# Normalised, transposed tokens of two segments kept in DRAM and read back, in place of making them a second time

## Chip, cores, metric

One core of one Trainium2 chip. The metric is the device time of one execution in microseconds (us), the median of several executions. A profile is of one execution of the same program and runs some 1.7 us shorter in its span than the measured time.

## The reference, cut to what matters

```python
x = A_x                                   # 2048 tokens x 1024
xn = _layernorm(x, axis=-1)
return x + _A_ref(xn, wq, wk, wv, wo, beta) + _B_ref(xn, w1, b1, w2, b2)
# A: 32 heads of 32; four segments of 512 tokens; in each, causal softmax attention
#    plus a read of a running memory M, z:  q, k, v = xn @ wq, xn @ wk, xn @ wv
# B: an MLP over the token axis: y = gelu(layernorm(xn)^T w1 + b1) w2 + b2
```

## The kernel before

The stages are: norm and first hidden products (to some 35 us), w1 (to some 180 us), w2 (to some 373 us) and attention (to the end). K of segments three and four is made in the w2 stage, between products of w2, from tokens that are scaled to f16 and transposed by DMA into `xnK`. In attention the same tokens are loaded from x, scaled and transposed again, in bf16, into `xnT`, for Q and V.

```python
def k_prepare(self, i, p):                       # called after each product of the w2 stage
    n = 7 * i + self.ORDER.index(p)
    if n in self.TOKENS_AT:                      # (2, 3, 4, 6, 8, 9, 10, 11)
        m = self.TOKENS_AT.index(n)
        c = 8 + m
        self.xn_scale(c, F16)
        self.fw.dma(self.xnK[m // 4][...], self.xs[c % 4][:].bitcast(F16), ..., transpose=True, own=True)
    if n - 2 in self.TOKENS_AT[:4]:
        self.xn_load(12 + self.TOKENS_AT.index(n - 2))
    n -= 7 * (self.K_FIRST - 1)
    if 1 <= n < 5:                               # the third of these overwrites half of xnK[1] in place
        self.differences(self.kB, self.R_kB, self.kD, self.R_kD, (n,))
    ...

def xn_load(self, c):                            # 256 KB of x
def xn_scale(self, c, dtype=BF16):               # DVE: (x - mean) * rstd, in place
def xn_transpose(self, c):                       # DMA transpose into xnT[s % 2]
```

Attention runs in 32 units. PE's work is cut into "dense" stretches (projections) between the logits and the weighing of the unit before; the DVE work of a unit is a queue of side steps, of which one is taken at certain stops of the dense stretches. When a job of eight matmuls is complete, `end(b)` empties its PSUM bank, and this too is mostly DVE work. Two banks alternate (6 and 7), so a job can't start before the job two back has been emptied.

```python
XN_AT = (0, 1, 2, 3, 6, 7, 8, 9, 14, 15, 16, 17)     # units with a token step
for u in range(N_UNIT):
    ...
    if u:
        self.weigh(u - 1, 2)
        self.side.append(...)                        # scales of unit u - 1
    if N_GRP <= u:
        self.side.append(lambda u=u: self.phi_q(u))
    self.side.extend(steps)                          # products, add, transpose of the output
    if u + 1 < N_UNIT:
        self.side.append(lambda u=u: (self.phi_k(u + 1), self.k_transpose(u + 1)))
    if xn is not None:
        self.side.append(lambda c=xn: (self.xn_scale(c), self.xn_transpose(c), ...))
    ...

def dense(self, n, side=True):
    ...                                              # matmuls of the job up to the next stop
        if stop == 8:
            end(b)                                   # e.g. kT <- PSUM, fin <- PSUM (DVE)
            self.jobs.popleft()
        elif self.side and stop in stops:
            self.side.popleft()()
```

Of the kernel before, what the change touches and what calls it, by code (L numbers as in the profile page):

```python
# [9 lines left out]
F16 = mybir.dt.float16  # L10
# [7 lines left out]
SEG_L = 512  # L18
F_MLP = 3584
P = 128  # L20
N_TCH = S_TOK // P
N_DCH = D_MODEL // P
# [364 lines left out]
class _Kernel:  # L387
# [508 lines left out]
    def alloc_w2_rest(self):  # L896
        w = _Walk(self.mem, self.B_AT + self.STG_AT, self.B_AT + self.S2_AT)
        self.stg, self.R_stg = [], []
        for k in range(4):
            t, r = w.take(f"stg{k}", [P, D_MODEL], BF16, 2)  # L900
            self.stg.append(t)
            self.R_stg.append(r)
        self.xs, self.R_xs = [], []
        self.take_xs(w, 1)
        w = _Walk(self.mem, self.B_AT + self.K_AT, self.B_AT + self.FREE_AT)
        self.take_xs(w, 3)
        self.wkp, self.R_wkp = [None] * 2, [None] * 2
        self.wkp[0], (self.R_wkp[0],) = w.take("wkp0", [P, N_DCH, 2 * P], BF16)
        self.sk, self.R_sk = w.take("sumk", [P, 4, N_DCH // 2, P], F16, 4)
        for k in range(2):  # L910
            self.load_stg(k)
        for m in range(4):
            self.xn_load(8 + m)
        self.alloc_w2(1)
        self.load_w2(1)
        self.load_wkp(0)
        w = _Walk(self.mem, self.B_AT + self.FREE_AT, self.SB_END - self.SB_BASE)
        self.xnK, self.R_xnK = [], []
        for k in range(2):
            t, r = w.take(f"xnK{k}", [P, N_DCH, SEG_L], F16, 4)  # L920
            self.xnK.append(t)
            self.R_xnK.append(r)
        self.kB = [[self.xnK[c][:, 4 * k:4 * k + 4, :] for c in range(2)] for k in range(2)]
        self.R_kB = [[self.R_xnK[c] for c in range(2)] for _ in range(2)]
        self.kD, self.R_kD = [], []
        for k in (0, 1, 3):
            t, r = w.take(f"kD{k}", [P, N_DCH // 2, SEG_L], F16)
            self.kD.append(t[:])
            self.R_kD.append(r)
        self.kD.insert(2, self.kB[0][1])  # L930
        self.R_kD.insert(2, self.R_kB[0][1])
        self.k_d = self.nc.dram_tensor("k_part", (N_UNIT // 2, P, SEG_L), BF16).ap()
        self.R_kd = [Res(f"kd{u}") for u in range(N_UNIT // 2)]
        self.pk_d = self.nc.dram_tensor("pk_part", (N_GRP, P, SEG_L), BF16).ap()
        self.R_pkd = [Res(f"pkd{u}") for u in range(N_GRP)]
# [105 lines left out]
    def k_prepare(self, i, p):  # L1041

        n = 7 * i + self.ORDER.index(p)
        if n in self.TOKENS_AT:
# [3 lines that stand above are left out]
            self.fw.dma(self.xnK[m // 4][:, :, (m % 4) * P:(m % 4 + 1) * P], self.xs[c % 4][:].bitcast(F16),  # L1048
                        reads=[self.R_xs[c % 4]], writes=[self.R_xnK[m // 4][m % 4]], transpose=True, own=True)
        if n - 2 in self.TOKENS_AT[:4]:  # L1050
            self.xn_load(12 + self.TOKENS_AT.index(n - 2))
        n -= 7 * (self.K_FIRST - 1)
        if 1 <= n < 5:
            self.differences(self.kB, self.R_kB, self.kD, self.R_kD, (n,))
        elif n == 5:
            self.alloc_kout()
        n, g = n % 7, n // 7
        if 0 <= g < self.N_KP and n == 6:
            self.pair_sums(("k", g), (1, 2))
        if i == self.N_W2 - 1 and n < 2:  # L1060
            for c in (2 * n, 2 * n + 1):
                self.xn_scale(c)
                self.xn_transpose(c)
# [57 lines left out]

    def put_out(self, c, t, R):
        self.fw.dma(self.part_d[:, c, :], t[:].bitcast(F16), reads=R, writes=[self.R_out[c]], is_output=True)

    def xn_load(self, c):
        self.fw.dma(self.xs[c % 4][:], self.x_d[:, c, :], writes=[self.R_xs[c % 4]])
# [141 lines left out]
    def proj_job(self, ring, u, end):  # L1268
        s = u // N_GRP

        def mm(b, i):
            self.fw.mm(self.bank(b), ring.slots[u % 2][:, i, :], self.xnT[s % 2][:, i, :], start=(i == 0), stop=(i == 7))

        def finish(b):
            if u + 2 < N_UNIT:
                ring.ensure(u + 2)
            end(b)

        return [0, None, lambda: [ring.res[u % 2]] + self.R_xnT[s % 2], mm, finish, ring is self.wk_ring]

    def v_job(self, m, c):
        s, bv, i = m // 2, m % 2, m % 3

        def mm(b, dc):
            self.fw.mm(self.bank(b), self.xnT[s % 2][:, dc, c * P:(c + 1) * P], self.wv[:, dc, bv * 512:(bv + 1) * 512],
                       start=(dc == 0), stop=(dc == 7))

        def end(b):
            dst, src = self.vA[i][:, c, :, 0:D_HEAD], self.bank(b).rearrange("p (h d) -> p h d", d=D_HEAD)
            if m in (1, 2):  # L1290
                self.fw.op("dve", lambda e: e.tensor_copy(dst, src), reads=[self.R_bank[b]], writes=[self.R_vA[i][c]])
            else:
                self.fw.op("act", lambda e: e.activation(dst, src, ACT.Copy), reads=[self.R_bank[b]],  # L1293
                           writes=[self.R_vA[i][c]])

        return [0, None, lambda: [self.R_wv[bv], self.R_xnT[s % 2][c]], mm, end, m in (1, 2)]

    def wo_job(self, c, half):
        s = c // 4
# [194 lines left out]
    QUOTA_FROM, QUOTA = 18, (24, 20)  # L1494
    STOPS = ((1, 4, 7), (1, 4))
    STOPS_FEW = ((1, 3, 5, 7), (1, 3, 5))
    XN_AT = (0, 1, 2, 3, 6, 7, 8, 9, 14, 15, 16, 17)

    def unit_jobs(self, u):
        jobs = [self.wo_job(*self.wo_jobs.popleft())] if 10 <= u < self.QUOTA_FROM else []  # L1500
# [22 lines left out]
    def attention(self):  # L1523
# [11 lines left out]
        for u in range(N_UNIT):  # L1535
            if u == N_GRP:
                t, R = _Walk(self.mem, self.B_AT + self.STG_AT, self.B_AT + self.S2_AT).take(
                    "oT2", [P, N_GRP, SEG_L], BF16, N_GRP)
                self.oT.append(t)
                self.R_oT.append(R)  # L1540
                self.load_fin(0)
                self.load_fin(1)
            if 1 <= u <= N_GRP:
                self.fw.dma(self.wo[:, u - 1, :], self.A_wo[(u - 1) * P:u * P, :], writes=[self.R_wo[u - 1]])
            even = u % 2 == 0
            self.jobs.extend(self.unit_jobs(u))
            total = 8 * len(self.jobs) - sum(j[0] for j in self.jobs) - self.left
            xn = self.XN_AT.index(u) + 4 if u in self.XN_AT else None
            if u in self.XN_AT[::4]:
                self.xn_load(xn)  # L1550
                self.xn_load(xn + 1)
            if u >= 18 and even:
                cuts = self.cut(total, (0, 5, 1, 4, 0, 9, 5))
            elif u < 10 or u >= 14 and total <= 26:
                cuts = self.cut(total, (0, 4, 2, 4, 1, 13, 8) if even else (7, 3, 2, 4, 1, 15))
            else:
                cuts = self.cut(total, (0, 4, 2, 2, 2, 14, 8) if even else (7, 3, 2, 2, 2, 16))
            end = u >= N_UNIT - 4
            self.stops = self.STOPS_FEW if total <= 26 and u >= 14 else self.STOPS
            self.dense(cuts[0])  # L1560
            self.logits(u, 0)
            self.dense(cuts[1], end)
            while end and self.side:
                self.side.popleft()()
            if u:
                self.weigh(u - 1, 0)
            self.dense(cuts[2], False)
            if u:
                self.weigh(u - 1, 1)
            self.dense(cuts[3], False)  # L1570
            if u:
                self.weigh(u - 1, 2)
                steps = self.combine(u - 1)
                last = steps[-1]
                steps[-1] = lambda u=u, last=last: (last(), self.o_transpose_dma(u - 1))
                self.side.append(steps.pop(0))
# [3 lines that stand above are left out]
                self.side.extend(steps)  # L1580
# [3 lines that stand above are left out]
                self.side.append(lambda c=xn: (self.xn_scale(c), self.xn_transpose(c), c % 4 < 2 and self.xn_load(c + 2)))  # L1584
            self.dense(cuts[4])
            self.logits(u, 1)
            if even:
                self.dense(cuts[5])
                self.logits(u, 2)
            self.dense(8 * len(self.jobs) - sum(j[0] for j in self.jobs) - self.left)  # L1590
# [87 lines left out]
```

## Time and profile before

| | before |
|---|---|
| time, median of 6 runs | 652.26 us (652.11 to 652.52) |
| PE busy, clock | 645.9 us, full |
| DVE busy | 433.7 us |
| DMA share, 200 to 250 us | 0.78 |
| DMA share, 450 to 500 and 500 to 550 us | 0.60, 0.69 |

PE is the bound nearly everywhere (94% of the chain that ended last); DVE comes next, with 41.6 and 43.8 us of 50 in two stretches of attention. The lines are in the prediction.

### The profile page before, as it was taken

To read this page: it belongs to the slowest core of one execution; us is meant where nothing else is said; L and a number is where in the kernel's file an instruction comes from. 1 tells how busy PE (TensorE), PEld (TensorE's weight loads), DVE (VectorE), ACT (ScalarE), POOL (GpSimd) and SP (SyncE) were. 2 spreads that over 40 slices of the span, in tenths; PEclk is the share of its full clock that TensorE was granted. 3 is DMA by queue.
4 is the path that set the end of the run, shared out by engine and by line. 5 is a ranking of instruction groups with operands and counts; after the bars stand their busy time and mean duration, and the time that the engine had idled before them with its cause. 6 is when DMAs were issued, how large, how long until landed. Compare 5 with 4: busy or idle time off the path is not lost.

```text
span 650.5 us, 11182 instructions
## 1 busy us (share of the span) xinstructions
PE 645.9 (99%) x4611; PEld 303.6 (47%) x4611; DVE 433.7 (67%) x808; ACT 281.4 (43%) x305; POOL 154.2 (24%) x179
## 2 busy tenths in 40 slices
PE   9999999999999999999999999999999999999998
PEld 3444444444444444444444444444544454445544
DVE  6975676665555664744638325767887888777896
ACT  7543232232210000111101047778767778889770
POOL 2500000000011220220202203343334444554440
PEclk9999999999999999999999999999999999999999
DMA  9804233242498947538262957979654677435434
GB/s 303 216 0 130 65 107 88 64 116 79 127 261 193 238 120 210 157 102 231 79 208 96 263 130 177 184 168 227 134 135 98 155 165 139 112 98 128 105 94 139
DMA packets 190123, 95.00 MB, mean 146 GB/s; under 512 B 108664, under 2 KB 176248, under 8 KB 190072
## 3 DMA queue, kind: packets, MB, share of 16 engines
q1 hardware_dynamic: 189928, 94.25, 57.2%
q8 instruction: 36, 0.59, 0.4%
q14 instruction: 15, 0.12, 0.1%
q10 hardware_dynamic: 144, 0.03, 0.0%
HBM read 69.23 MB, written 11.53 MB: 124 GB/s over the span
## 4 chain that ended last, share of the span: by engine, by line
PE 94%; DVE 3%; ACT 2%; issue 1%; DMA 0%; POOL 0%; DVEq 0%
PE ps_all L199 94%; ACT pT L1364 1%; DVE prod L1465 1%; DVE ln_st L587 1%; DMA xin<-in_A_x_dram 0%; DVE h L627 0%; DVE ost L1418 0%; POOL ln_rs L611 0%; DVE mtmp L1230 0%; DVE kT L1262 0%; DVE fin L1307 0%; DVE mtmp L1228 0%; ACT qT L1253 0%; ACT vA L1293 0%; DVE ln_mv L590 0%
## 5 line engine op out<-in xcount | busy, mean ns | idle before, releaser
L1364 ACT ACTIVATE pT<-ps_all 128x2048 bf16<-128x2048 f32 x80 | 150.2, 1877 | 47.4 <-PE ps_all L199 46.9
L1368 POOL TENSOR_SCALAR_AFFINE_SELECT pT<-pT 128x512 bf16<-128x512 bf16 x128 | 105.6, 843 | 160.7 <-ACT pT L1364 160.7
L689 DVE TENSOR_TENSOR part<-ps_all,part 128x512 f32<-128x512 f32 x84 | 57.7, 690 | 108.2 <-PE ps_all L199 87.8
L1075 POOL TENSOR_TENSOR part<-part,stg 128x512 f32<-128x512 f32 x24 | 33.0, 1404 | 285.1 <-DVE part L689 285.1
L199 PE MATMUL ps_all<-wv,xnT 128*128 128x512 bf16 x256 | 68.5, 380 | 0.4 <-ACT qT L1253 0.2
L746 ACT ACTIVATE g<-part,b1c 128x512 f16<-128x512 f32 x36 | 26.0, 722 | 98.8 <-DVE part L689 98.8
L199 PE MATMUL ps_all<-xnT,wq 128*128 128x512 bf16 x256 | 66.4, 380 | 0.0
L199 PE MATMUL ps_all<-wo,oT 128*128 128x512 bf16 (+2 forms) x272 | 63.8, 367 | 0.0
L694 ACT ACTIVATE part<-ps_all 128x512 f32<-128x512 f32 x24 | 14.0, 596 | 101.1 <-PE ps_all L199 67.1
L1418 DVE TENSOR_TENSOR ost<-ps_all,eps 128x396 bf16<-128x396 f32 (+1 forms) x72 | 37.2, 522 | 28.5 <-PE ps_all L199 27.8
L199 PEld LDWEIGHTS ps_all<-vA,pT 128*128 128x128 bf16 x1280 | 45.7, 96 | 20.4 <-DVE ost L1418 1.7
L199 PE MATMUL ps_all<-g,sum 128*128 128x512 f16 x224 | 51.0, 379 | 0.0
L199 PE MATMUL ps_all<-g,w2s 128*128 128x512 f16 x224 | 51.0, 379 | 0.0
L199 PE MATMUL ps_all<-gT,sum 128*128 128x512 f16 x224 | 50.3, 379 | 0.0
L199 PE MATMUL ps_all<-vA,pT 128*128 128x33 bf16 x1280 | 48.5, 177 | 0.3 <-DVE ost L1418 0.3
L199 PE MATMUL ps_all<-h,sum 128*128 128x512 f16 x192 | 45.2, 379 | 0.0
L199 PE MATMUL ps_all<-h,w1s 128*128 128x512 f16 x192 | 44.9, 379 | 0.0
L199 PE MATMUL ps_all<-hT,sum 128*128 128x512 f16 x192 | 43.6, 379 | 0.0
L199 PEld LDWEIGHTS ps_all<-wo,oT 128*128 128x128 bf16 x272 | 23.9, 98 | 24.4 <-issue 3.7
L199 PEld LDWEIGHTS ps_all<-xnT,wq 128*128 128x128 bf16 x256 | 22.6, 97 | 25.4 <-issue 5.3
L199 PEld LDWEIGHTS ps_all<-g,sum 128*128 128x128 f16 x224 | 21.9, 98 | 26.4
L199 PEld LDWEIGHTS ps_all<-g,w2s 128*128 128x128 bf16 x224 | 21.9, 98 | 26.4
(118 smaller groups left out, 875.1 us busy)
## 6 DMA issues: line engine op xcount, KB each, us to landing
w2s<-in_B_w_dram SPq DMA_DIRECT2D x8, 1792.0 KB, 9.5
w1s<-in_B_w_dram SPq DMA_DIRECT2D x12, 1024.0 KB, 5.6
wq<-in_A_wq_dram SPq DMA_DIRECT2D x32, 256.0 KB, 3.3
xs<-in_A_x_dram SPq DMA_DIRECT2D x24, 256.0 KB, 3.4
stg<-in_A_x_dram SPq DMA_DIRECT2D x16, 256.0 KB, 2.9
out_dram<-stg SPq DMA_DIRECT2D x16, 256.0 KB, 3.9
wk<-in_A_wk_dram SPq DMA_DIRECT2D x16, 256.0 KB, 3.6
fin<-out_dram SPq DMA_DIRECT2D x16, 256.0 KB, 3.2
```

Of the source, the lines that this page charges most:

```text
L199: ins = self.nc.tensor.matmul(*args, **kwargs)
L587: fw.op("dve", lambda e: e.bn_stats(st[:, 6 * h:6 * h + 6], src[:, 512 * h:512 * h + 512]), reads=[self.R_xin[c]], writes=[R])
L689: self.fw.op("dve", lambda e: e.tensor_tensor(self.tmp[dst][:], self.bank(b), self.tmp[src][:], op=ALU.add), reads=[self.R_bank[b], self.R ...
L694: self.fw.op("act", lambda e: e.activation(self.tmp[dst][:], self.bank(b), ACT.Copy), reads=[self.R_bank[b]], writes=[self.R_tmp[dst]])
L746: self.fw.op("act", lambda e: e.activation(self.gB[f % 2][half][:, f // 2, :], src, ACT.Gelu_apprx_tanh, bias=self.b1c[:, f:f + 1], scale= ...
L1075: fw.op("pool", lambda e: e.tensor_tensor(self.tmp[t][:], self.tmp[t][:], self.stg[k][:, 512 * half:512 * half + 512], op=ALU.add), reads= ...
L1364: fw.op("act", lambda e: e.activation(dst, src, ACT.Exp, scale=SCALE), reads=self.R_bank[0:4], writes=[R[v % 2][kb] for v, kb, _ in blocks ...
L1368: fw.op("pool", lambda e: e.affine_select(d, d, pattern=[[0, 4], [1, P]], compare_op=ALU.is_ge, fill=0.0, base=0, channel_multiplier=-1), ...
L1418: fw.op("dve", lambda e: e.tensor_tensor(dst, src, eps, op=ALU.add), reads=[self.R_bank[b], self.R_eps], writes=[self.R_ost[o][part]])
L1465: fw.op("dve", lambda e: e.tensor_tensor(self.prod[:], ost[:, :, 0:D_HEAD], rec.unsqueeze(2).to_broadcast([P, 32, D_HEAD]), op=ALU.mult), ...
```

## The change

The intent is to make the tokens of the last two segments once. They lie in `xnK` in f16 already; the change writes them to DRAM (two writes of 1 MB) and replaces eight loads, eight scales and eight DMA transposes of the attention phase by eight plain loads. Q and V of these segments then read f16 tokens against bf16 weights.

```diff
+        if n in (9, 13):
+            k = (n - 9) // 4
+            self.fw.dma(self.xn_d[k], self.xnK[k][:], reads=self.R_xnK[k], writes=[self.R_xnd[k]], is_output=True)
...
+    def xn_of(self, s):
+        t = self.xnT[s % 2][:]
+        return t.bitcast(F16) if s >= 2 else t
+
+    def xn_part(self, s, k):
+        self.fw.dma(self.xn_of(s)[:, 2 * k:2 * k + 2, :], self.xn_d[s - 2, :, 2 * k:2 * k + 2, :], reads=[self.R_xnd[s - 2]],
+                    writes=[self.R_xnT[s % 2][k]], own=True)
...   (q and v jobs read self.xn_of(s) in place of self.xnT[s % 2])
-            if u in self.XN_AT[::4]:
+            if xn == 4:
                 self.xn_load(xn)
                 self.xn_load(xn + 1)
+            for k in (1, 2):
+                if u in self.XN_AT[k]:
+                    self.xn_part(k + 1, self.XN_AT[k].index(u))
```

More of the change, by code (lines that the diff above doesn't have):

```diff
@@ L932, in alloc_w2_rest @@
         self.k_d = self.nc.dram_tensor("k_part", (N_UNIT // 2, P, SEG_L), BF16).ap()
+        self.xn_d = self.nc.dram_tensor("xn_part", (2, P, N_DCH, SEG_L), F16).ap()
+        self.R_xnd = [Res(f"xnd{k}") for k in range(2)]
         self.R_kd = [Res(f"kd{u}") for u in range(N_UNIT // 2)]
@@ L1271, in mm @@
         def mm(b, i):
-            self.fw.mm(self.bank(b), ring.slots[u % 2][:, i, :], self.xnT[s % 2][:, i, :], start=(i == 0), stop=(i == 7))
+            self.fw.mm(self.bank(b), ring.slots[u % 2][:, i, :], self.xn_of(s)[:, i, :], start=(i == 0), stop=(i == 7))
         def finish(b):
@@ L1284, in mm @@
         def mm(b, dc):
-            self.fw.mm(self.bank(b), self.xnT[s % 2][:, dc, c * P:(c + 1) * P], self.wv[:, dc, bv * 512:(bv + 1) * 512],
+            self.fw.mm(self.bank(b), self.xn_of(s)[:, dc, c * P:(c + 1) * P], self.wv[:, dc, bv * 512:(bv + 1) * 512],
                        start=(dc == 0), stop=(dc == 7))
@@ L1294, in end @@
                            writes=[self.R_vA[i][c]])
-        return [0, None, lambda: [self.R_wv[bv], self.R_xnT[s % 2][c]], mm, end, m in (1, 2)]
+        return [0, None, lambda: [self.R_wv[bv]] + (self.R_xnT[s % 2][c:c + 1] if s < 2 else self.R_xnT[s % 2]), mm, end, m in (1, 2)]
     def wo_job(self, c, half):
@@ L1496 @@
     STOPS_FEW = ((1, 3, 5, 7), (1, 3, 5))
-    XN_AT = (0, 1, 2, 3, 6, 7, 8, 9, 14, 15, 16, 17)
+    XN_AT = ((0, 1, 2, 3), (6, 7, 8, 9), (14, 15, 16, 17))
     def unit_jobs(self, u):
@@ L1547, in attention @@
             total = 8 * len(self.jobs) - sum(j[0] for j in self.jobs) - self.left
-            xn = self.XN_AT.index(u) + 4 if u in self.XN_AT else None
-            if u in self.XN_AT[::4]:
+            xn = self.XN_AT[0].index(u) + 4 if u in self.XN_AT[0] else None
+            if xn == 4:
                 self.xn_load(xn)
                 self.xn_load(xn + 1)
+            for k in (1, 2):
+                if u in self.XN_AT[k]:
+                    self.xn_part(k + 1, self.XN_AT[k].index(u))
             if u >= 18 and even:
```

## The prediction

> **What bounds the kernel now.** I read the page's table of busy time first, then the chain that ended last, then a table of stretches of 50 us, then the waits, and last the timeline of the two places that the change touches.
>
> ```profile
> PE 645.9 (99%) x4611; PEld 303.6 (47%) x4611; DVE 433.7 (67%) x808; ACT 281.4 (43%) x305; POOL 154.2 (24%) x179
> ...
> PEclk9999999999999999999999999999999999999999
> ...
> PE 94%; DVE 3%; ACT 2%; issue 1%; DMA 0%; POOL 0%; DVEq 0%
> ...
> L199 PE MATMUL ps_all<-g,sum 128*128 128x512 f16 x224 | 51.0, 379 | 0.0
> L199 PE MATMUL ps_all<-g,w2s 128*128 128x512 f16 x224 | 51.0, 379 | 0.0
> ...
> L199 PEld LDWEIGHTS ps_all<-g,sum 128*128 128x128 f16 x224 | 21.9, 98 | 26.4
> L199 PEld LDWEIGHTS ps_all<-g,w2s 128*128 128x128 bf16 x224 | 21.9, 98 | 26.4
> ```
>
> PE is busy 99% of the span, at the full clock, and 94% of the last chain is PE. The last four lines say something that the change needs: a moving operand in f16 takes the same 379 ns against f16 weights (sum) as against bf16 weights (w2s), and f16 weights load in the same 98 ns as bf16 ones.
>
> The stretches say where PE has any room (columns: stretch, its length, then busy us of PE, PEld, DVE, ACT, POOL, then clock, DMA share, GB/s):
>
> ```profile
> 200.00:250.00 50.00, 50.00 (x234) 22.68 (x232) 29.54 (x35) 2.39 (x4) 8.46 (x6) 1.00 0.78 198
> ...
> 400.00:450.00 50.00, 50.00 (x572) 24.97 (x573) 33.98 (x82) 39.37 (x34) 19.37 (x27) 1.00 0.90 180
> 450.00:500.00 50.00, 49.84 (x501) 24.03 (x500) 41.56 (x84) 37.38 (x36) 18.44 (x23) 1.00 0.60 137
> 500.00:550.00 50.00, 49.81 (x582) 25.27 (x582) 43.84 (x85) 40.25 (x36) 23.71 (x26) 1.00 0.69 152
> ```
>
> The first is the w2 stage beside K, where the writes are added; the other three are the part of the attention phase where the work is taken away. PE idles 0.35 us in the three together. Since a busy PE may still hide short waits, I also summed, over the records, the time from one matmul's start to the next one's less its columns at 2.4 per ns: about 21 us of excess from 350 us to the end, of which some 17 us are the 0.1 us steps into and out of the 32-row logits matmuls, whose number does not change. Single waits above 0.25 us there are only six, 1.8 us together. So all that a faster DVE or DMA could give back is 2 to 4 us of 650.
>
> **What the Trainium skill says.** "TensorE: Matmul & The Clock Gate", section "Back-to-back issue gap", gives N/2.4 + 2.5 ns for a lone warm matmul, 215.8 ns at 512 columns. The trace agrees: groups of 14 such matmuls follow each other every 3.02 us in the w2 stage, 215.7 ns each. (Its faster "sustained" figure of 131 ns is not seen here.) "Perfetto Trace Analysis", section "Identifying the Most-Contended Engine", warns that matmul busy share is no measure of distance to the roofline; hence the check by starts above. "VectorE: DVE Perf Modes", section "The perf-mode tier table", puts tensor_scalar on 16-bit SBUF data in its fastest tier, 693 ns for 2048 elements; here 1024 elements take 543 ns, with f16 or bf16 output alike. "DMA: Bandwidth & Descriptors", section "Measured", has 1 MB in 6.15 us; here the 1024 KB w1s loads land in 5.6 us (median), and the 1792 KB w2s loads in 9.5.
>
> **The change, part by part.** The static order of the two kernels shows the same PE, ACT and POOL instructions in the same order. DVE loses eight instructions and two others move by a place; SP loses six.
>
> 1. Removed from attention: eight DVE scales of xs, 8 x 0.543 = 4.3 us, of DVE's 119 us in 400 to 550. The two places where DVE does hold PE are these:
>
> ```profile
> 482.09 0.69 DVE L1230 SCALAR_TENSOR_TENSOR mtmp<-kT,mtmp 128x512 bf16<-128x512 bf16 x1
> 482.70 0.68 DVE L1262 CAST kT<-ps_all 128x512 bf16<-128x512 f32 x1
> 483.30 1.03 DVE L1418 TENSOR_TENSOR ost<-ps_all,eps 128x396 bf16<-128x396 f32 x2
> ```
>
> The weighing on PE at 483.91 waits 0.3 us for ost, and the same at 503.18. The last scale before them ran at 468.33 and the next at 510.12; after 490.87 DVE even idled 2.25 us before ost. So the scales are not in those queues, and the 4.3 us fall almost wholly beside PE. I give it 0.2 us.
>
> 2. Removed: eight loads of x (256 KB) and eight DMA transposes (256 KB, 1.24 to 2.11 us of SP each); added: eight plain loads of 256 KB. No PE wait in 400 to 550 is put down to a DMA, so this is worth 0 us, maybe 0.1.
>
> 3. Added: two writes of 1 MB in the w2 stage. Here is the queue as it stands, and the DVE steps that depend on it:
>
> ```profile
> 218.48 4.62 SPq L221 DMA_TRANSPOSE xnK<-xs  x3
> 223.15 0.58 SPq L221 DMA_DIRECT2D out_dram<-stg  x1
> 223.78 0.44 SPq L221 DMA_DIRECT2D w2s<-in_B_w_dram  x1
> 224.26 4.42 SPq L221 DMA_DIRECT2D out_dram<-stg  x1
> ```
> ```profile
> 229.35 1.21 DVE L663 TENSOR_TENSOR kD<-xnK,xnK 128x2048 f16<-128x2048 f16 x1
> ...
> 238.70 2.17 DVE L663 TENSOR_TENSOR xnK<-xnK 128x2048 f16<-128x2048 f16 x1
> ...
> 241.45 1.08 DVE L648 TENSOR_TENSOR sum<-sum,w2s 128x1792 f16<-128x1792 f16 x1
> ```
>
> The 16 DMA engines are 0.9 to 1.06 busy from 180 to 230, moving some 240 GB/s, so 1 MB costs about 4.4 us of all of them (an estimate from that rate). The first write goes between the first and second of the last three transposes: the last tokens land near 229.5 in place of 225, just when the difference at 229.35 wants them. The w2s load issued at 223.78 lands 8.5 us later, at 232.3; now near 236.7, ahead of its first reader on DVE at 237.4 and on PE at 243.7. The second write is queued behind it, and lands near 239 to 241. The difference at 238.70 overwrites half of the second xnK in place, so it must now wait for that write to have read it: 0 to 2.5 us. After it, PE next needs a sum made at 241.45 to 242.5, at 247.54 (5 us of room), and the sums for K that end at 247.8, at 250.56 (2.8 us of room). So the expected stall of DVE fits into the room, and PE pays 0; if the write lands 3 to 4 us later than I think, PE pays 1 or 2 us. I give it 0.2 us on average.
>
> 4. Changed type: 128 q matmuls (16 units x 8) get an f16 moving operand with bf16 weights, as g with w2s has: no cost. 128 v matmuls get f16 weights with a bf16 moving operand, a pair that the trace does not have; both types alone are free, so I take 0 us. Sum: -0.2 - 0.1 + 0.2 = -0.1 us.
>
> **The rivals.** (a) The freed DVE and DMA time comes through: waits of ACT and DVE shrink and PE's small gaps close. For it: DVE is at 83 to 88% in 450 to 550. Against: the gaps are 2 to 4 us in all, and those above 0.25 us from 555 on lie after the last removed item (538). It would give 650.5 to 651.5. (b) The writes become a new wait: DMA is the fullest resource just where they are put, and the in-place difference is tied to the second one. PE would stop for 1 to 4 us around 247 to 252: 653.5 to 656. (c) The mixed types cost something at each switch between bf16 logits or weighings and f16 projections, some 6 switches in each of 16 units; at 20 ns, 2 us: 654.5. Nothing in the trace speaks for it, and the f16 stage shows nothing when weights alternate between f16 and bf16. (d) The plain loads must wait for PE to be done with the old tokens and hold up the transposes of oT and pk behind them on SP: each has about a unit (8 us) of room, so I think it hidden.
>
> **Range and chances.** The three runs of before spread by 0.36 us. Rival (a) sets the lower edge, (b) and (c) the upper, which I think somewhat likelier to be touched. A gain of 2% is 13 us, more than all PE waits of the phase, so faster is nearly out of the question; slower by 2% needs a cost of 0.1 us in each of the 128 v matmuls or a wait repeated unit by unit. Predicted 652.3 us, range 650.8 to 654.8; faster 0.01, same 0.96, slower 0.03.
>
> **What would show it.** PE's busy time stays at about 645 us with the same count of matmuls; DVE's falls by 4 to 5 us; the q and v matmuls stay at 380 ns and their starts 216 ns apart; xs has 16 scales in place of 24. In the w2 stage a DVE wait on the second write may appear before the in-place difference, up to 3 us, with no PE wait behind it. I am wrong if PE idles near 247 to 252, if v matmuls with f16 weights start more than 220 ns apart, if PE's clock falls below full, or if a wait on the loads from the kept copy appears at the first v or q job of segments three and four.

## The result, and the profile after

652.6 us median (652.43 to 652.84, 6 runs) against 652.26 us: a ratio of 1.0005, 95% interval 0.9992 to 1.0018. Ratios are the mean time of one kernel's fast runs over that of the other's of the same rounds, so not quite the ratio of the medians.

First the page's busy line of the changed kernel, and its stretches (columns as before):

```profile
PE 645.8 (99%) x4611; PEld 303.2 (47%) x4611; DVE 428.1 (66%) x800; ACT 281.4 (43%) x305; POOL 153.9 (24%) x179
```
```profile
200.00:250.00 50.00, 50.00 (x234) 22.65 (x232) 29.99 (x36) 2.39 (x4) 8.46 (x6) 1.00 0.89 239
...
450.00:500.00 50.00, 49.71 (x504) 24.09 (x501) 39.23 (x81) 37.64 (x37) 17.77 (x23) 1.00 0.50 123
500.00:550.00 50.00, 49.81 (x568) 24.80 (x566) 40.92 (x81) 40.24 (x36) 24.41 (x26) 1.00 0.55 133
```

The work did move: DVE lost 5.6 us, the DMA share fell from 0.60 to 0.50 and from 0.69 to 0.55 where the tokens were made, and rose from 0.78 to 0.89 where they are written. PE did not notice: 645.8 us.

The w2 stage, where I had feared a stall, in the timeline of the changed kernel (start, length, engine, line, operation, tiles):

```profile
231.04 0.32 SPq L221 DMA_DIRECT2D xn_part<-xnK  x1
```
```profile
229.62 1.22 DVE L663 TENSOR_TENSOR kD<-xnK,xnK 128x2048 f16<-128x2048 f16 x1
...
238.96 2.17 DVE L663 TENSOR_TENSOR xnK<-xnK 128x2048 f16<-128x2048 f16 x1
```

Both differences stand 0.27 us later than before, and the whole timeline was shifted by as much since 183 us, before the first write, by a wait of PE on DVE that comes and goes between runs. Behind it stands a w2s load issued at 170 us, which neither kernel changes: in all fourteen profiles PE's first weights of `gT` with `sum` are loaded 5.16 to 5.17 us after it lands, and it lands at 177.87 to 178.50 us (178.05 here before, 178.31 after). So up to 0.6 us between single executions is chance, from this load alone. No wait is shown before either difference. The writes landed 5.5 us after issue (median of the two, the longer 6.0), so the second was through by about 237. The last tokens landed at 226.2 us and the w2s load behind them at 234.1, later than before by 1.3 and 1.8 us.

The changed kernel's profile is 0.6 us longer than the other's. 0.27 us is that shift. The other 0.3 us are here, at 472 us; DVE and PE of the kernel before, then of the changed one:

```profile
472.17 0.68 DVE L1262 CAST kT<-ps_all 128x512 bf16<-128x512 f32 x1
...
473.57 0.59 PE L199 MATMUL ps_all<-wo,oT 128*128 128x512 bf16 x2
```
```profile
472.47 1.00 DVE L1243 SCALAR_TENSOR_TENSOR mtmp<-kT,mtmp 128x512 bf16<-128x512 bf16 x1
...
473.39 0.68 DVE L1275 CAST kT<-ps_all 128x512 bf16<-128x512 f32 x1
...
474.12 0.11 PEld L199 LDWEIGHTS ps_all<-wo,oT 128*128 128x128 bf16 x2 [0.42 <-DVE kT L1275]
474.13 0.61 PE L199 MATMUL ps_all<-wo,oT 128*128 128x512 bf16 x2
```

With one side step fewer in the queue, phi of k was taken one stop earlier, and the copy that empties a bank fell in behind it. It ran 1.2 us later (0.27 of it the shift), and PE waited for the bank: between the start of the last wv matmul and the first wo one lie 0.52 us where 0.22 us stood.

To see whether such a wait lasts to the end, I compared the start of each of PE's 4611 weight loads with the same one of the kernel before. The changed kernel falls behind for good at two places only, by 0.27 us at 182 to 183 us and by 0.31 us at 473.6, and is 0.54 us behind at its last weight load. So the 0.3 us aren't made good later.

### The profile page after: what moved, and what is told of

Same layout as the page of the kernel before. It is cut to its first block, busy times and chain, and to the rows that moved or that the text cites. A ratio compares the mean times of both kernels' runs of the same rounds, so it can differ in the third digit from the quotient of the medians.

```text
span 651.1 us, 11170 instructions
## 1 busy us (share of the span) xinstructions
PE 645.8 (99%) x4611; PEld 303.2 (47%) x4611; DVE 428.1 (66%) x800; ACT 281.4 (43%) x305; POOL 153.9 (24%) x179
## 4 chain that ended last, share of the span: by engine, by line
PE 91%; DVE 5%; ACT 2%; DMA 2%; issue 1%; POOL 0%; DVEq 0%
PE ps_all L199 91%; ACT pT L1377 1%; DMA w2s<-in_B_w_dram 1%; DVE prod L1478 1%; DVE ln_st L587 1%; DVE sum L648 0%; DMA xin<-in_A_x_dram 0%; DVE mtmp L1243 0%; DVE h L627 0%; DVE mtmp L1241 0%; DVE fin L1320 0%; DVE ost L1431 0%; DVE kT L1275 0%; POOL ln_rs L611 0%; DVE part L689 0%
## 5 line engine op out<-in xcount | busy, mean ns | idle before, releaser
L199 PE MATMUL ps_all<-xnT,wq 128*128 128x512 bf16 (+1 forms) x256 | 66.4, 380 | 0.0
L199 PEld LDWEIGHTS ps_all<-gT,sum 128*128 128x128 f16 x224 | 21.8, 98 | 26.8 <-DVE gT L663 0.6
```

The costliest lines, as they stand in the source:

```text
L199: ins = self.nc.tensor.matmul(*args, **kwargs)
```

## The experiments

Kernels are compared only within the same rounds. Where 0.3 us is at stake, the interval of the ratio (about 0.0013 to either side, 0.85 us) cannot carry a verdict; there I rest on single waits in the trace and say so. By the rule of 2% every run here is "the same" as the kernel before; where I write "slower", the interval lies above 1.

### Its place in the queue kept (e1_place), and the pair repeated (after_again, e1_again)

```diff
             if xn is not None:
                 self.side.append(...)
+            elif u in self.XN_AT[1] + self.XN_AT[2]:
+                self.side.append(lambda: None)
```

> The changed kernel, but an empty step stands in the side queue where each removed scale stood, so that DVE's order is that of the kernel before less eight scales (checked: no other difference in order). In the changed kernel one copy of kT out of PSUM slipped behind two other DVE steps and ran at 473.39 where it ran at 472.17 before, and PE waited 0.31 us for that bank at 473.8. Theory (the slipped copy is the cost): the copy is back before those steps, the wait near 474 is gone, and the time is 0.3 us below the changed kernel, 652.2 to 652.4, equal to the kernel before. Rival (the writes or the mixed types cost it): the wait may go, but the time stays at 652.6.

> The changed kernel itself once more, beside the next three on one chip, since 0.3 us is as large as the spread of single runs. Theory (a slipped copy of kT costs 0.3 us): 652.5 to 652.8, 0.2 to 0.4 above the same kernel with its places kept, and the wait of 0.3 us near 474 again. Rival (the 0.3 us was chance): the two within 0.1.

> The changed kernel with its places kept in the side queue, a second time, on the same chip as the changed kernel. Theory: 652.3 within 0.15, equal to the kernel before and 0.2 to 0.4 below the changed kernel. Rival: no difference to the changed kernel.

e1_place: 652.43 us, against 652.36 for the kernel before (ratio 1.0001, 0.9988 to 1.0014). On one chip: the changed kernel 652.61 us (652.49 to 652.86), with the place kept 652.37 us (652.16 to 652.65), the kernel before 652.38 us. In the timeline of e1_place the copy is in front again and the wait is gone:

```profile
472.00 0.68 DVE L1275 CAST kT<-ps_all 128x512 bf16<-128x512 f32 x1
...
473.68 0.59 PE L199 MATMUL ps_all<-wo,oT 128*128 128x512 bf16 x2
```

after_again has the wait a second time:

```profile
473.71 0.11 PEld L199 LDWEIGHTS ps_all<-wo,oT 128*128 128x128 bf16 x2 [0.43 <-DVE kT L1275]
```

The wait is in both traces of the changed kernel and in neither of the two with the place kept. By the starts of weight loads against the kernel before, after_again falls behind by 0.30 us at 473.6 us, and it keeps this to the end; the two with the place kept have no step there and end within 0.06 us of the kernel before. So the slipped copy, which e1 takes away alone, costs PE 0.3 us, and no other cost of the change is seen on PE. (The spans of the four profiles don't show this: 651.1 and 650.7 us for the changed kernel, 650.9 for both with the place kept. The latter two are each the slowest of five executions and took 0.3 us longer behind PE's last work.) The medians fit with 0.2 to 0.3 us, but their intervals overlap.

### The writes alone (e2_writes)

The kernel before with the two writes added in `k_prepare`, and nothing that reads them.

```diff
+        if n in (9, 13):
+            k = (n - 9) // 4
+            self.fw.dma(self.xn_d[k], self.xnK[k][:], ..., is_output=True)
```

> The kernel before with the two 1 MB writes alone; the attention phase is untouched and nobody reads what is written. Theory (the writes fit into the room that DVE and PE have): 652.3, as before, within 0.2, no PE wait between 215 and 260, and the same DVE times to within 0.5 us. Rival (the writes are the cost): 652.6 or more, with a DVE wait before the in-place difference near 239 or a later w2s load that holds DVE.

652.33 us against 652.36 (ratio 0.9999, 0.9987 to 1.0012). The in-place difference began at 238.55 in place of 238.70, with no wait. So two writes cost no time. There was little room to spare: in this execution the second write landed at 238.0 us, half a us before the difference that has to wait for it.

### The types alone (e3_types)

The kernel before, with the eight scales writing f16 and q and v reading `xn_of(s)`.

```diff
-(self.xn_scale(c), self.xn_transpose(c), ...)
+(self.xn_scale(c, F16 if c >= 8 else BF16), self.xn_transpose(c), ...)     # and xn_of(s) in q_job, v_job
```

> The kernel before with tokens of segments three and four scaled to f16 and used as f16 by q and v; loads, scales and transposes stay. Theory (types are free): 652.3 within 0.2; the q and v matmuls of these segments 379 ns, starts 216 ns apart inside a group, weights loaded in 98 ns. Rival (a switch between bf16 and f16 costs some ns): with 20 ns at some 100 switches 2 us more, 654.

652.3 us against 652.36 (ratio 0.9998). The view of the token tile of e3_types shows both pairs of types in one group (nanoseconds are least, median, most):

```profile
L199 PE MATMUL ps_all<-xnT,wq x256: 376/379/390, 373.6 to 617.5; 128*128 128x512 bf16 x64, 128*128 128x512 f16 x64
L199 PEld LDWEIGHTS ps_all<-wv,xnT x256: 95/98/99, 376.9 to 600.8; 128*128 128x128 bf16 x64, 128*128 128x128 f16 x64
L199 PE MATMUL ps_all<-wv,xnT x256: 376/379/390, 377.1 to 601.0; 128*128 128x512 bf16 x128
```

The first two groups are half of each type, and half of the third has f16 weights under its bf16 operand; the spread is 14 ns for matmuls and 4 ns for loads. Starts inside a group follow at 216 ns (median) in v and q, as before. The types cost nothing here.

### The saving alone (e4_loads)

Wrong result: raw x is loaded straight into the token tile, without writes, scales, transposes or f16. (Its output still passed the comparison; so that comparison does not see the attention branch of these segments well.)

```diff
+    def xn_part(self, s, k):
+        self.fw.dma(self.xnT[s % 2][:, 2 * k:2 * k + 2, :]..., self.x_d[:, 4 * s + k, :], ...)
-                self.side.append(lambda c=xn: (self.xn_scale(c), self.xn_transpose(c), ...))     # for c >= 8
+                self.side.append(lambda: None)
```

> WRONG RESULT ON PURPOSE: the eight loads, scales and transposes in attention are replaced by eight plain 256 KB loads of raw x straight into the token tile, in bf16, with empty steps keeping DVE's order; no writes, no f16. The saving of the change alone, without any of its costs. Theory (the removed work lay beside PE): 652.1 to 652.4, at most 0.2 us below before; DVE busy falls by 4.3 us and PE's waits at 483 and 503 stay at 0.3 us each. Rival (the saving is real and the writes or types ate it): 651.5 or less.

652.28 us against 652.36 (ratio 1.0, 0.9986 to 1.0014), with DVE at 428.7 us in place of 433.7. The waits at 483 and 503 are where they were (0.33 us each by matmul starts). So nothing was gained and then eaten: the removed work was never in the time.

### How much room DVE has: copies added (e5_copies1, e5_copies3)

The kernel before, with one or three copies of the token tile onto itself ahead of each of the eight scales.

```diff
+        for _ in range(m if c >= 8 else 0):
+            self.fw.op("dve", lambda e: e.tensor_copy(x[:], x[:]), reads=[R], writes=[R])
```

> The kernel before with three more copies of the token tile onto itself at each of the eight scales of segments three and four: what the change takes away on DVE, fourfold in place of none, 8 x 3 x 0.54 = 13 us more of DVE. Theory (one scale fits into DVE's room of about 1 us, but not four): at the scale at 468 the copy of kT slips by 1.6 us and PE waits some 0.8 us; over all places 1 to 4 us more, 653.3 to 656.3. Rival (DVE has room to spare anywhere): within 0.3 us of before. Rival (DVE work goes into the time one for one): 13 us more, 665.

> The kernel before with one extra copy (some 0.45 us) at each of the eight scales, in place of three, which cost 8.2 us. Theory (a queue with some 0.5 to 1 us of room at each place: what fits costs nothing, what exceeds it costs one for one): the waits of the threefold run, less two copies each, leave 0.2 to 1.2 us: 652.5 to 653.6. Rival (each us of DVE costs 0.6 to 0.8 us from the first on, so that taking the scales away should also have gained): 8 x 0.45 x 0.75 = 2.7 us, 655.

| kernel | DVE busy, us | time, us |
|---|---|---|
| place kept, scales gone (e1_again) | 428.7 | 652.37 |
| before | 433.7 | 652.38 |
| one copy more at each | 437.0 | 653.13 |
| three copies more at each | 444.8 | 660.53 |

The threefold run missed my 653.3 to 656.3: it cost 8.1 us. I had looked at one of the eight places. The list of PE's waits in e5_copies3 shows that three different evacuations came late (us in total, times, longest):

```profile
PE ps_all L199 <- DVE ost L1423: 2.9, 5, 1.1
PE ps_all L199 <- DVE kT L1267: 2.3, 2, 1.7
PE ps_all L199 <- DVE fin L1312: 1.6, 3, 1.0
```

The seven new waits end at 458, 460, 478, 518, 531, 535 and 550 us, so they stand at most of the places and not at one. The single copy then met its forecast (0.2 to 1.2 us expected, 0.7 found against 652.43 us; the interval, 0.9999 to 1.0024, only just takes in 1). By the starts of weight loads 0.40 us of it stand at 473.6, before the same wo matmul that the slipped copy held. The curve bends just above the place where the tuned kernel stands: 5 us of DVE less give nothing, 3.3 us more cost 0.7, the next 7.8 cost 7.4.

### How much room the w2 stage has: writes doubled and trebled (e6_writes2, e6_writes3)

The kernel of e2_writes with each 1 MB written two or three times, to places of their own.

```diff
-            self.fw.dma(self.xn_d[k], self.xnK[k][:], ...)
+            for j in range(m):                       # m = 2, 3
+                self.fw.dma(self.xn_d[m * k + j], self.xnK[k][:], ...)
```

> The kernel before with each of the two 1 MB writes made twice, to separate places. Theory (single writes fit, with at least 3 us to spare): one more MB ahead of the last two transposes and the w2s load moves them by 3.5 to 4.5 us, and DVE's first difference from 229 to 231 to 233; PE loses 0 to 2 us: 652.3 to 654.3. Rival (DMA traffic here is hidden whatever its size): 652.3, no shift on DVE.

> The same with each write three times, 4 MB more than the change writes. Theory: the w2s load that PE needs at 243 lands some 8 us later than with one write, near or after that time, the in-place difference waits for the last write as well, and PE loses 3 to 10 us: 655 to 662. Rival (hidden): 652.3.

Twice: 652.54 us against 652.43 (ratio 1.0001, 0.9986 to 1.0017). Three times: 657.87 us (ratio 1.0088, 1.0074 to 1.0101). DVE of the first, then DVE and PE of the second, in their timelines:

```profile
242.88 1.23 DVE L663 TENSOR_TENSOR xnK<-xnK 128x2048 f16<-128x2048 f16 x1 [3.86 <-DMA xn_part<-xnK]
```
```profile
248.59 1.23 DVE L663 TENSOR_TENSOR xnK<-xnK 128x2048 f16<-128x2048 f16 x1 [8.25 <-DMA xn_part<-xnK]
...
250.63 1.87 PE L199 MATMUL ps_all<-xnK,wkp 128*128 128x512 f16 x4 [3.33 <-DVE stg L1089]
252.29 5.34 PE L199 MATMUL ps_all<-gT,sum 128*128 128x512 f16 x14
```
```profile
245.00:260.00 15.00, 11.67 (x41) 4.58 (x40) 10.16 (x14) 1.19 (x2) 0.00 (x0) 0.77 0.63 191
```

The wait I had drawn is real, and its size is a matter of dose: none with one write, 3.86 us of DVE with two, which its room swallows almost whole, 8.25 us with three, of which 3.33 reach PE. (3.86 us is more than the 2.8 us of room that I had drawn. But the late difference took 1.23 us, where it takes 2.17 beside POOL's add, so what follows it on DVE was only 3.2 us late, and PE fell behind by 0.3 us at 249 to 251.) The first DVE difference did not move at two writes (229.60), against my forecast for it. At three writes the forecast of the time held, but the w2s load landed at 239.2, 4.7 us later than with one write and not 8, so PE's stop came from the late in-place difference and the evacuation behind it.

At three there is a second price. After its wait PE needed 5.34 us for fourteen matmuls that take 3.19 us otherwise, starting 427 ns apart until 256.6 us and 216 ns again from 257, and the clock of the stretch was 0.77: after the stop PE ran for some 6 us at about half its clock. The profile is of the slowest of the four executions (659.23 us); their mean clocks were 0.995, 1.0, 0.997 and 0.997, so the price was not the same in all, and what the one at 1.0 (657.75 us) lost instead isn't shown. "TensorE: Matmul & The Clock Gate", section "What's actually happening", says that the gate falls to half after an idle window of about 3.4 us; this run's stop of 3.33 us agrees with that, and none of the shorter waits of e5_copies3, 1.9 us at most, shows it. Where between 1.9 and 3.33 us the limit lies no run here shows.

### A version from what was found (e7_held, e8_held11)

PE waits 0.3 us at 483 and 503 for `ost`, which stands behind phi of k on DVE, in the shorter of the two intervals between weighings. Phi of k of some units is held back into the next, longer one; the place is kept as in e1.

```diff
-                self.side.append(lambda u=u: (self.phi_k(u + 1), self.k_transpose(u + 1)))
+                step = lambda u=u: (self.phi_k(u + 1), self.k_transpose(u + 1))
+                (held if u in (11, 13) else self.side).append(step)      # e8: u == 11
...
+                if held:                                                 # in the next unit, ahead of its first step
+                    steps[0] = lambda first=held.pop(), then=steps[0]: (first(), then())
```

> The changed kernel with places kept, and the step that makes phi of k and its transpose held back in units 11 and 13 and done at the head of the next unit's side work: it takes 1.0 us of DVE work out of the short stretch before each of the two weighings for which PE waits at 483 and 503, and puts it into the long stretch after, where DVE idles 2.25 us. Theory (these two waits are DVE's queue): both waits of 0.3 us vanish, 651.7 to 651.9, a little below both kernels. Rival (something else ends the waits, or they return at the next step): 652.3.

> The changed kernel with places kept, and the phi of k held back in unit 11 alone: of the earlier trial with units 11 and 13 the first half, without the second, behind which the evacuation fin fell in behind the 1.65 us product step and stopped PE for 1.79 us. Theory: the wait of 0.3 us at 483 is gone, the one at 503 stays, nothing new: 652.0 to 652.15, 0.3 below the kernel with places kept. Rival (the room comes back as a wait at the next step that PE meets): 652.3 to 652.4.

e7_held: 653.42 us against 652.38 (ratio 1.0016, 1.0002 to 1.0029): slower, so the forecast of 651.7 to 651.9 missed. Both waits went, but in the unit after 13 this came instead:

```profile
506.99 1.65 DVE L1478 TENSOR_TENSOR prod<-ost,srec 128x1024 bf16<-128x1024 bf16 x1
...
508.56 0.68 DVE L1320 TENSOR_TENSOR fin<-ps_all,fin 128x512 bf16<-128x512 f32 x1
...
509.52 1.03 PE L199 MATMUL ps_all<-wv,xnT 128*128 128x512 bf16 x4 [1.79 <-DVE fin L1320]
```

It is the slipped copy over again: the pushed-back product ran ahead of an evacuation that PE needed. The starts of weight loads account for the result: 0.30 us gained at 484, 0.34 at 503, 1.68 lost at 508. With unit 11 alone, e8_held11 took 651.86 us (651.71 to 652.22) against 652.43 for the kernel before (652.24 to 652.66), ratio 0.9993, interval 0.998 to 1.0005. Its timeline at the place, DVE and PE:

```profile
482.43 0.57 DVE L1431 TENSOR_TENSOR ost<-ps_all,eps 128x396 bf16<-128x396 f32 x1
...
483.52 0.56 PE L199 MATMUL ps_all<-vA,pT 128*128 128x33 bf16 x16
```

Before, `ost` began at 483.30 and the weighing at 483.91. The forecast was 652.0 to 652.15, so it came out a little lower; the trace accounts for 0.3 us (by weight loads 0.33 at 483.9), the rest is within the spread. It is the fastest median of all, but by 0.09%, and the interval takes in 1, so no gain is shown by the times.

## Why the prediction was right

The forecast was 652.3 us, 650.8 to 654.8, the same at 0.96; measured 652.6. The mechanism held: PE is the bound, and what was moved lies beside it. In the sum of -0.1 us, the gain of 0.2 and the cost of 0.2 both came out as 0; that they cancelled is luck. The 0.3 us that came was in no term.

- **Its first step, PE as the bound with 2 to 4 us to be had at most, held.** e4_loads has the whole saving and no cost, and gained 0.1 us within a spread of 0.4.
- **Removed DVE work, "8 x 0.543 = 4.3 us", was mis-sized, without harm.** The eight scales took 5.85 us in the kernel before: three of 0.54 us and five of 0.79 to 0.88. I took the median of all 24. In the trace the five long ones overlap a mask of POOL in time and the three short ones do not, and each long one ends 0.27 to 0.28 us after the mask that it met. "SBUF — State Buffer", section "SBUF: two separate sides", describes a port pair that DVE and GpSimd hold in turn for a whole instruction; that agrees with these ends.
- **The gain of 0.2 us from it was not seen.** The reason given, that the scales are not in the queues that hold PE, was right: the two waits at 483 and 503 stayed.
- **DMA work in attention, 0 to 0.1 us: right.** The share fell by 0.10 to 0.14 and no time with it.
- **The writes: right in the sum (0), too dark in the way.** I had the second landing near 239 to 241 and DVE waiting 0 to 2.5 us; it landed by about 237 and DVE did not wait. The term that was mis-sized is "1 MB costs about 4.4 us of all of them": what stood behind the first write came 1.3 and 1.8 us later, and the DMA share from 200 to 250 us rose by 0.11, some 2.8 us of all engines for each MB (an estimate from the two shares). The room I drew (5 and 2.8 us) was about right: a wait of 3.86 us cost 0.1 us between the medians, 0.3 in the profile.
- **Types, 0: right, by a run of their own.** (Rival (c) is summed a little high: 96 switches of 20 ns are 1.9 us, 654.2 and not 654.5.)
- **What the sum left out is a term, not a size.** The text says that "two others move by a place" on DVE, and prices that at nothing. One of the two was the copy of kT that empties a bank, which fell behind two other steps, and it is the only cost of the change that any trace shows: 0.3 us. The range was wide enough that this omission could not make the forecast wrong. The listing of both orders had it before any run; I should have asked for each moved instruction whether PE waits for it.
- **Rivals.** (a) falls with e4_loads, (b) with e2_writes as far as one write goes, (c) with e3_types. (d) is not seen: no wait on the read-back loads stands before any q or v job, and with the place kept PE's weight loads stay within 0.21 us of those of the kernel before from 200 us to the end. None of the four signs of being wrong appeared either: PE was busy throughout 240 to 260 us, v matmuls with f16 weights start 216 ns apart (median), the clock was full, and no such wait stood.

What stays open: the 0.3 us are shown on PE in two executions of the changed kernel, and the medians agree with them, but the spread of single executions is as large, part of it from the w2s load at 178 us. And why a write of 1 MB delays what is behind it by less than its bytes at 240 GB/s isn't shown.

## What to carry to other kernels

In a kernel like this one, whose bound engine is busy 99% of the time, work taken from the others is worth what they make it wait, not what they spend; a run with the whole saving and none of its costs tells that at once. But the room of the second engine is not symmetric: here 5 us less gave nothing, and 11 us more cost 8. So when a step leaves a queue that several kinds of work share, look at what closes up behind it: a copy that empties a bank two steps later can cost more than the removed step was worth.

## What the Trainium skill lacked or had wrong

- "TensorE: Matmul & The Clock Gate", section "Back-to-back issue gap": its sustained 131 ns per matmul at 512 columns was not seen in any run; groups follow at 215.7 ns each (14 in 3.02 us), its figure for a lone one, and the closest two starts in all fourteen traces are 214 ns apart.
- The same page has nothing on mixed 16-bit types: bf16 weights with an f16 moving operand, and f16 weights with a bf16 one, both took 379 ns a matmul and 98 ns a load, as pure bf16 does.
- "VectorE: DVE Perf Modes", section "The perf-mode tier table", gives one time for each operation and none for it beside POOL; the same tensor_scalar of 1024 elements took 0.54 us alone, 0.79 to 0.88 us while POOL was masking and 1.37 us beside POOL's add of 2.0 us.
- No page that I read says how long a 1 MB write from SBUF to DRAM takes: 5.5 us from issue to landing beside other traffic, 6.7 and 8.0 us (medians) when two or three were queued at once.
